# First pair's queries fetched from ScalarE's queue beside its keys; the gate values fetched and computed behind them

## The chip, the core and the metric

The kernel runs on one core of a Trainium2 chip. The metric is device time in microseconds (us), the median of several runs. An engine is named as in the profile: PE (TensorE), DVE (VectorE), ACT (ScalarE), POOL (GpSimd) and SP (SyncE), of which SP only issues transfers here. ACT can issue transfers too, between its computations.

## What is computed

One attention layer (4 batches, 8 heads, 576 positions, 64 wide) with a memory term and a gate for each head, and behind it two feed-forward layers with 2,304 tokens, 512 to 2,048 to 512.

```python
def _attn_ref(q, k, v, M_prev, z_prev, beta):
    scores = scale * np.matmul(q, k.transpose(0, 1, 3, 2))     # causal mask, softmax -> a
    local = np.matmul(a, v)
    q_p = phi(q)
    mem_out = einsum('bhsd,bhde->bhse', q_p, M_prev) / (einsum('bhsd,bhd->bhs', q_p, z_prev)[..., None] + 1e-06)
    g = 1.0 / (1.0 + np.exp(-beta))[None, :, None, None]
    return g * mem_out + (1 - g) * local
# then x @ w_in -> elu -> @ w_out, then x @ w2_in -> leaky relu -> @ w2_out
```

## The kernel before

**Work.** A pair is two heads of one batch, so there are 16 pairs, four to a batch. For each pair the kernel loads keys, queries and values as natural rows (`load_qk`, `load_rest`; tiles `kn`, `qn`, `vn`, one buffer each), transposes keys and queries on PE (`k_unit` line 294, `q_unit` line 312), and copies them out of PSUM on ACT (lines 296 and 241) and DVE (line 243). Two head-items of a pair, each in two groups of rows (chunks 0 and 1, then 2 to 4), go through scores (PE line 426, in later batches 428 and 429), mask and row minimum (DVE 431), exponential (ACT 436), normalisation (POOL 445 and 451, DVE 446), transposes of the weights (PE 457, copied out by ACT into `d`, `ah`, `ac`), and the product with the values (PE 524). `phi_unit` makes the memory term from `qn` (ACT 385 and 386, DVE 387, POOL 389 and 396); it needs `ging`, and POOL 451 needs `omg`, both made from the gate input `beta`. The first batch is computed in full-precision matmuls, the others in split high and low parts.

**Weights.** The feed-forward weights come as 64-bit numbers (`wraw`, lines 103 and 107, 512 KB each, two buffers) and are decoded by ACT (113, later 127), DVE (114 to 122, later 128 to 132), an ACT cast (241, `w`) and a subtraction. Seven blocks of the first layer are decoded beside the first batch's attention.

**Filling.** When a batch is done, its feed-forward part (PE 620 and 648) is laid between the attention units of the next batch. After the last attention unit the rest of it, the remaining weight blocks and then the second half of layer one and layer two follow. At that handover `u_x` makes the input of the next part: DVE adds the two halves (681), ACT rounds them in four pieces (`xh`, 610), POOL makes the remainders (`xl`, 613). PE's first matmul on that part waits for one ACT count, that of the fourth piece.

**Order.** The code writes units in a fixed order, and a scheduler then orders the instructions of each engine, once, when the program is built. Transfers carry one of eight counters in turn (printed `DMAHW0` to `DMAHW7`), and a transfer waits until the one before it on its counter has landed. So a transfer that moves at the start renumbers those behind it.

**Start.** SP issues `beta`, four transfers of keys, four of queries, then values and weights. ACT loads its function table and makes `ging` (line 84); DVE makes `ging`, `gat`, `omg` (85 to 87).

Of the kernel before, what the change touches and what calls it, by code (L numbers as in the profile page):

```python
# [11 lines left out]
AF = mybir.ActivationFunctionType  # L12
ALU = mybir.AluOpType
AX = mybir.AxisListType

P = 128
# [8 lines left out]
def kernel(  # L25
# [14 lines left out]
    nc = tc.nc  # L40
# [38 lines left out]
    bet = const.tile([P, H], F32, name="bet")  # L79
    gat = const.tile([P, H], F32, name="gat")  # L80
    ging = const.tile([P, H], F32, name="ging")
    omg = const.tile([P, H], F32, name="omg")
    nc.sync.dma_start(bet, beta.partition_broadcast(P))
    nc.scalar.activation(out=ging, in_=bet, func=AF.Exp, scale=-1.0)
    nc.vector.tensor_scalar(out=ging, in0=ging, scalar1=1.0, scalar2=None, op0=ALU.add)
    nc.vector.reciprocal(gat, ging)
    nc.vector.tensor_scalar(out=omg, in0=gat, scalar1=-1.0, scalar2=1.0, op0=ALU.mult, op1=ALU.add)


    wi_tiles = {}  # L90
    wo_tiles = {}
# [57 lines left out]
    def halves(n):  # L149
# [18 lines left out]
        out=mask[:, 448:576], in_=mask[:, 448:576], pattern=[[-1, 128]], compare_op=ALU.is_ge,  # L168
# [37 lines left out]
    def bank(tag):  # L206
        return psum.tile([P, 512], F32, tag=tag, bufs=BANKS[tag], name=tag)

    def load_rows(dst, src, b, hp, dup):

        hs = slice(2 * hp, 2 * hp + 2)
        for ca, cb, r0 in ((0, 2 if dup else 3, 0), (3, 5, 320)):
            for j in range(2):
                nc.sync.dma_start(
                    dst[:, ca:cb, j * D:(j + 1) * D],
                    src[b, 2 * hp + j, r0:r0 + (cb - ca) * P, :].rearrange("(c p) d -> p c d", p=P),
                )
        for r in range(2 if dup else 0):
            nc.sync.dma_start(
                dst[64 * r:64 * r + 64, 2, :].rearrange("p (j d) -> p j d", j=2),  # L220
                src[b, hs, 256:320, :].rearrange("j p d -> p j d"),
            )
# [29 lines left out]
    class Pair:  # L252
# [12 lines left out]
        def load_qk(self):  # L265
            self.q = at.tile([P, 5, P], F32, tag="qn", bufs=1, name="qn")
            self.k = at.tile([P, 5, P], F32, tag="kn", bufs=1, name="kn")
            load_rows(self.k, k, self.b, self.hp, False)
            load_rows(self.q, q, self.b, self.hp, False)

        def load_rest(self):
            b, hp = self.b, self.hp
            self.v = at.tile([P, 5, P], F32, tag="vn", bufs=1, name="vn")
            load_rows(self.v, v, b, hp, True)
            if hp % 2 == 0:
                load_memory(b, 2 * hp)
            zb, mr = memory_in[b, hp]
            h0 = 2 * (hp % 2)
            self.z = zb[:, h0 * D:h0 * D + P]
            self.mr = mr[:, h0:h0 + 2, :]  # L280
# [262 lines left out]
    def weave(*lists):  # L543

        keyed = []
        for n, (kind, l) in enumerate(lists):
            keyed += [((i + 0.5) / len(l) + SHIFT[kind], n, i, u) for i, u in enumerate(l)]
        return [u for _, _, _, u in sorted(keyed, key=lambda e: e[:3])]

    def attention_units():  # L550

        pairs = [Pair(ti, hp) for ti in range(len(tiles1)) for hp in range(NHP)]
        keys = [(pr, j, g) for pr in pairs for j in range(2) for g in pr.groups]
        items = [Item(*key, n) for n, key in enumerate(keys)]
        first = {}
        for n, it in enumerate(items):
            first.setdefault(id(it.pr), n)
        units = [(0, pairs[0].load_qk, None), (0, pairs[0].load_rest, None)]
        def prep(pi):
            pr = pairs[pi]  # L560
            l = [(PC, lambda g=g: pr.k_unit(g)) for g in pr.kgroups]
            l += [(PC, lambda g=g: pr.q_unit(g)) for g in pr.groups]
            l += [(0, pr.phi_unit)]
            if pi + 1 < len(pairs):
                l.append((0, pairs[pi + 1].load_qk))
            return l

        units += [(c, u, None) for c, u in prep(0)]
        for n in range(len(items) + 2):
            lists = []  # L570
            if n < len(items):
                it = items[n]
                pr = it.pr
                pi = pairs.index(pr)
                head = []
                if first[id(pr)] == n:
                    head.append((0, pr.v_unit))
                    if pi + 1 < len(pairs):
                        head.append((0, pairs[pi + 1].load_rest))
                if n + 1 < len(items) and items[n + 1].pr is not pr:  # L580
                    lists.append(("prep", prep(pi + 1)))
                lists.append(("score", head + it.stages()[0]))
            if 1 <= n <= len(items):
                lists.append(("tr", items[n - 1].stages()[1]))
            if n >= 2:
                it = items[n - 2]
                c = list(it.stages()[2])
                if first[id(it.pr)] == n - 2:
                    c = [(PC, lambda g=g, pr=it.pr: pr.qp_unit(g)) for g in it.pr.groups] + c
                lists.append(("pv", c))  # L590
            w = weave(*lists)
            done = None
            if n >= 2 and (n == len(items) + 1 or items[n - 1].pr.ti != items[n - 2].pr.ti):
                done = items[n - 2].pr.ti
            units += [(c, u, None) for c, u in w[:-1]] + [(w[-1][0], w[-1][1], done)]
        return units
# [143 lines left out]
    def close_mlp():  # L740
# [9 lines left out]
        NW, NG, EB = TW, 3, 2  # L750

    att = attention_units()
    n0 = [d for _, _, d in att].index(0) + 1
    c0 = sum(c for c, _, _ in att[:n0])
# [198 lines left out]
```

## Time and profile before

| what | value |
|---|---|
| median of 3 runs | 1080.63 us (1078.21 to 1080.70) |
| profiled execution | 1078.67 us, of which the span is 1076.9 us |
| PE busy | 1042.8 us, 97% of the span |
| DVE, ACT, POOL busy | 55%, 45%, 49% |
| transfers | 115.05 MB, mean 107 GB/s |

Times in the rows further down are microseconds from the span's start. In a timeline row the first number is the start and the second the duration; a bracket at the end gives how long the engine stood idle before it and who released it. In a row of a stretch, each engine has its busy time and, in parentheses, its instructions; then come the clock granted to PE (1.00 is full), the mean busy share of the transfer engines, and GB/s.

### The profile page before, as it was taken

The page shows a single profiled execution, that of the slowest core. Times are in us where ns is not written, and L with a number is a line of the kernel's source. Part 1 is how long each engine was busy: PE and PEld are TensorE (multiplying, and loading weights), DVE is VectorE, ACT ScalarE, POOL GpSimd, SP SyncE. Part 2 cuts the span into 40 slices and gives each one's busy share as a digit, 9 for nine tenths or more (in the row PEclk, how much of TensorE's full clock was granted, in tenths as well). Part 3 has the DMA queues.
Part 4 walks back from the last instruction along what each step waited for, and adds up shares of the span by engine and source line. Part 5 has one row for each costly group of instructions (what it writes and reads, how often), then busy time and mean ns, then how long its engine had stood idle before and what let it go on. Part 6 is the DMA issues. An engine that isn't in the chain of part 4 may idle for free.

```text
span 1076.9 us, 17323 instructions
## 1 busy us (share of the span) xinstructions
PE 1042.8 (97%) x5904; PEld 912.1 (85%) x5904; DVE 589.7 (55%) x1382; ACT 484.3 (45%) x1169; POOL 529.9 (49%) x674
## 2 busy tenths in 40 slices
PE   6998999999999998999999999999999999999997
PEld 3776799989999998988888889888888888888896
DVE  6889987788878647566672214654322221232232
ACT  5999877778877634544442224432211211111111
POOL 6676775677667525654542225954422422222221
PEclk9999999999999998999999999999999999999999
DMA  7755553564446247765671304430200100000010
GB/s 182 197 145 117 161 142 101 122 169 145 114 120 161 90 134 240 251 226 179 201 224 61 117 1 134 160 118 1 79 1 1 59 20 1 10 30 1 1 40 20
DMA packets 150408, 115.05 MB, mean 107 GB/s; under 512 B 80048, under 2 KB 142000, under 8 KB 150320
## 3 DMA queue, kind: packets, MB, share of 16 engines
q1 hardware_dynamic: 150320, 113.94, 35.9%
q8 instruction: 47, 0.77, 0.3%
q14 instruction: 41, 0.34, 0.1%
HBM read 78.52 MB, written 31.85 MB: 102 GB/s over the span
## 4 chain that ended last, share of the span: by engine, by line
PE 81%; DVE 8%; DMA 5%; ACT 2%; issue 2%; POOL 1%; SPq 1%; DVEq 0%; POOLq 0%; ACTq 0%
PE pm L620 18%; PE tp L620 15%; PE sc L901 14%; PE sc L648 10%; PE pm L648 4%; PE po L901 4%; PE tp L457 3%; PE po L524 3%; PE po L648 3%; PE pm L524 2%; DVE pt L431 2%; PE sc L426 1%; DMA y<-xq 1%; PE sc L428 1%; PE sc L429 1%
## 5 line engine op out<-in xcount | busy, mean ns | idle before, releaser
L627 POOL TENSOR_TENSOR gl<-e,gh 128x512 fp32r<-128x512 f32 (+2 forms) x181 | 200.8, 1112 | 384.5 <-DVE gh L243 267.4
L620 PE MATMUL tp<-xw,w 128*128 128x512 f32 (+1 forms) x504 | 144.3, 367 | 0.0
L620 PE MATMUL pm<-xw,w 128*128 128x512 f32 (+1 forms) x496 | 141.9, 369 | 0.0
L901 PE MATMUL sc<-w,gh 128*128 128x512 f32 x448 | 135.9, 390 | 0.0
L451 POOL TENSOR_SCALAR pt<-pt,rs,omg 128x128 f32<-128x128 f32 (+4 forms) x160 | 102.1, 647 | 22.1 <-DVE rs L446 17.9
L620 PEld LDWEIGHTS tp<-xw,w 128*128 128x128 f32 x504 | 91.8, 188 | 16.1
L648 PE MATMUL sc<-gh,w 128*128 128x512 f32 (+2 forms) x438 | 104.8, 340 | 0.0
L620 PEld LDWEIGHTS pm<-xw,w 128*128 128x128 f32 x496 | 90.6, 188 | 16.3
L436 ACT ACTIVATE pt<-pt,mx 128x128 f32<-128x128 f32 (+4 forms) x160 | 93.3, 585 | 17.2 <-DVE mx L431 16.3
L901 PEld LDWEIGHTS sc<-w,gh 128*128 128x128 f32 x448 | 83.1, 188 | 16.5
L620 PE MATMUL tp<-xv,w 128*128 128x512 f32 (+1 forms) x252 | 92.6, 367 | 0.0
L620 PE MATMUL pm<-xv,w 128*128 128x512 f32 (+1 forms) x248 | 91.4, 369 | 0.0
L639 ACT ACTIVATE e<-pm 128x512 f32<-128x512 f32 (+1 forms) x40 | 22.2, 555 | 143.2 <-PE pm L620 140.2
L457 PE MATMUL tp<-ident,pt 128*128 128x128 f32 x480 | 81.6, 279 | 2.8 <-ACT ah L247 0.9
L901 PE MATMUL sc<-w,gl 128*128 128x512 f32 x224 | 84.3, 389 | 0.0
L640 DVE TENSOR_TENSOR e<-tp,e 128x512 f32<-128x512 f32 (+1 forms) x40 | 25.5, 637 | 106.3 <-ACT e L639 106.3
L648 PEld LDWEIGHTS sc<-gh,w 128*128 128x128 f32 x438 | 74.8, 188 | 8.6
L138 POOL TENSOR_TENSOR w<-wm,w 128x512 fp32r<-128x512 f32 x50 | 65.5, 1331 | 33.1 <-ACT w L241 22.1
L640 DVE TENSOR_TENSOR e<-pm,e 128x512 f32<-128x512 f32 (+1 forms) x40 | 25.5, 637 | 101.8 <-ACT e L639 101.8
L620 PE MATMUL pm<-xh,w 128*128 128x288 f32 x368 | 80.6, 306 | 0.3 <-DVE e L634 0.3
L243 DVE CAST gh<-e 128x512 fp32r<-128x512 f32 (+2 forms) x146 | 72.9, 503 | 12.7 <-PE po L901 2.2
L639 ACT ACTIVATE e<-tp 128x512 f32<-128x512 f32 (+1 forms) x40 | 22.1, 554 | 117.7 <-PE tp L620 112.2
(157 smaller groups left out, 2444.1 us busy)
## 6 DMA issues: line engine op xcount, KB each, us to landing
wraw<-in_moe_w_in_dram SPq DMA_DIRECT2D x32, 512.0 KB, 4.0
wraw<-in_moe_w_out_dram SPq DMA_DIRECT2D x32, 512.0 KB, 5.2
xh<-xh SPq DMA_DIRECT2D x8, 576.0 KB, 3.1
xl<-xl SPq DMA_DIRECT2D x8, 576.0 KB, 3.8
ys<-st SPq DMA_DIRECT2D x32, 144.0 KB, 2.8
x<-x1s SPq DMA_DIRECT2D x9, 512.0 KB, 3.9
out_dram<-st SPq DMA_DIRECT2D x36, 128.0 KB, 1.7
vn<-in_v_dram SPq DMA_DIRECT2D x64, 64.0 KB, 2.3
```

The source lines that it names most:

```text
L138: nc.gpsimd.tensor_tensor(out=w[:, 1, a], in0=t[:, a], in1=_f(w)[:, 0, a], op=ALU.subtract)
L243: (nc.vector if eng == "V" else nc.gpsimd).tensor_copy(dst, src)
L436: nc.scalar.activation(out=pt[0:m, 0:nk], in_=pt[0:m, 0:nk], func=AF.Exp, scale=-1.0, bias=mx[0:m, last:last + 1], accum_out=self.pd["ss"] ...
L451: nc.gpsimd.tensor_scalar(out=pt, in0=pt, scalar1=rs[0:m, i:i + 1], scalar2=omg[0:m, h:h + 1], op0=ALU.mult, op1=ALU.mult,)
L457: nc.tensor.transpose(dst, self.p[c][:, k0:k0 + kn], ident)
L524: nc.tensor.matmul(po[:, a:b], w, x, start=i == 0, stop=i == len(mms) - 1)
L620: nc.tensor.matmul(ph, wi[:, wj, kc, :], xx[:, kc, :], start=n_mm == 0, stop=n_mm == 11)
L627: nc.gpsimd.tensor_tensor(out=gl, in0=g, in1=_f(gh), op=ALU.subtract)
L639: nc.scalar.mul(t, ph, 0.01)
L640: nc.vector.tensor_tensor(out=t, in0=ph, in1=t, op=ALU.max)
L648: nc.tensor.matmul(py, wo[:, wj, ec * P:(ec + 1) * P], gg, start=opens and f == first and n_mm == 0, stop=closes and f == last and n_mm == 2,)
L901: nc.tensor.matmul(pos[tb], gg[:, tb * P:(tb + 1) * P], wo[:, wj, :], start=f == 0 and n_mm == 0, stop=f == NF - 1 and n_mm == 2,)
```

## The change

`load_rows` takes the issuing engine as an argument, and the first pair's queries use ACT's. The gate block becomes a function, which the list of units calls between `load_qk` and `load_rest` of the first pair. No arithmetic is added or removed, and every engine has the instructions it had, except that four transfers go from SP to ACT. Since line numbers move by one behind the gate block, line 215 of the kernel after is line 214 of the kernel before, and so on.

```diff
-    nc.sync.dma_start(bet, beta.partition_broadcast(P))
-    nc.scalar.activation(out=ging, in_=bet, func=AF.Exp, scale=-1.0)
-    nc.vector.tensor_scalar(out=ging, in0=ging, scalar1=1.0, scalar2=None, op0=ALU.add)
-    nc.vector.reciprocal(gat, ging)
-    nc.vector.tensor_scalar(out=omg, in0=gat, scalar1=-1.0, scalar2=1.0, op0=ALU.mult, op1=ALU.add)
-
+
+    def gates():
+        nc.sync.dma_start(bet, beta.partition_broadcast(P))
...
-    def load_rows(dst, src, b, hp, dup):
+    def load_rows(dst, src, b, hp, dup, eng=nc.sync):
...
-                nc.sync.dma_start(
+                eng.dma_start(
...
-            load_rows(self.q, q, self.b, self.hp, False)
+            load_rows(self.q, q, self.b, self.hp, False, nc.sync if self.ti or self.hp else nc.scalar)
...
-        units = [(0, pairs[0].load_qk, None), (0, pairs[0].load_rest, None)]
+        units = [(0, pairs[0].load_qk, None), (0, gates, None), (0, pairs[0].load_rest, None)]
```

The scheduler puts out another order from the start on, on every engine, up to the early part of what follows the attention; PE's order is the same from its instruction 3,389 of 5,786 on.

First place: SP at the start of the program. Before:

```order
L83 DMA bet<-in_beta_dram 128x8
L214 DMA kn<-in_k_dram 128x3x64 x2
L214 DMA kn<-in_k_dram 128x2x64 x2
L214 DMA qn<-in_q_dram 128x3x64 x2
L214 DMA qn<-in_q_dram 128x2x64
L214 DMA qn<-in_q_dram 128x2x64 [waits DMAHW0_49]
L214 DMA vn<-in_v_dram 128x2x64 [waits DMAHW1_49]
L103 DMA wraw<-in_moe_w_in_dram 128x4x256 [waits DMAHW2_49]
```

SP at the same place, after:

```order
L215 DMA kn<-in_k_dram 128x3x64 x2
L215 DMA kn<-in_k_dram 128x2x64 x2
L85 DMA bet<-in_beta_dram 128x8 [waits DMAHW0_49]
L104 DMA wraw<-in_moe_w_in_dram 128x4x256 [waits DMAHW1_49]
L108 DMA wraw<-in_moe_w_out_dram 128x1024 [waits DMAHW2_49]
L215 DMA vn<-in_v_dram 128x2x64 [waits DMAHW3_49]
```

The queries have left SP; `beta` now waits on the counter of the first query transfer (counters 0 and 3 are those that the first query transposes on PE wait for), and the weights stand ahead of the values. PE's transposes of query chunks 0 to 2 now stand between those of key chunks 0 to 2 and those of key chunks 3 and 4; before, all keys came first.

Second place: ACT where it first copies transposed weights `ah` out of PSUM, some 27 us into the span before. In it, `po<-wraw` opens the decoding of half a weight block and `CAST w` ends it. Before:

```order
L113 ACTIVATE po<-wraw 128x512 [waits DMAHW2_49,DVE_49]
L436 ACTIVATE pt_515,ss_149<-pt_515,mx 128x128 [waits DVE_49,Pool_49]
L436 ACTIVATE pt_526,ss_149<-pt_526,mx 128x256 [waits DVE_49,Pool_49]
L241 CAST w_391<-po 128x512 [waits DVE_49]
L247 COPY ah<-tp 128x320 [waits PE_49] x2
```

ACT at the same copies, after:

```order
L529 COPY xp<-pm 64x256 [waits PE_49]
L114 ACTIVATE po<-wraw 128x512 [waits DMAHW2_49,DVE_49]
L248 COPY ah<-tp 128x320 [waits PE_49] x2
L463 COPY d_146<-tp 128x384 [waits PE_49]
L242 CAST w_391<-po 128x512 [waits DVE_49]
```

The two copies of `ah` now stand ahead of the cast that ends that half block.

Third place: ACT at the handover behind the attention, some 400 us into the span. Before:

```order
L241 COPY st<-sc 128x288 [waits DMAHW2_49,PE_49]
L241 COPY st<-sc 128x288 [waits DMAHW4_49,PE_49]
L610 CAST xh_6579<-x 128x288 [waits DMAHW3_49,DMAHW7_49,DMAHW1_49,DVE_49]
L610 CAST xh_6579<-x 128x288 [waits DVE_49] x2
L127 ACTIVATE wm<-wraw 128x1024 [waits DMAHW5_49,DMAHW6_49,DMAHW2_49,DMAHW1_49]
L241 COPY st<-sc 128x288 [waits DMAHW0_49,PE_49,Activation_49]
L241 COPY st<-sc 128x288 [waits DMAHW1_49,PE_49,Activation_49]
L610 CAST xh_6579<-x 128x288
L241 CAST w_6660<-wm 128x1024 [waits DVE_49]
```

ACT at the same handover, after:

```order
L611 CAST xh_6579<-x 128x288 [waits DMAHW3_49,DMAHW7_49,DMAHW1_49,DVE_49]
L611 CAST xh_6579<-x 128x288 [waits DVE_49] x2
L128 ACTIVATE wm<-wraw 128x1024 [waits DMAHW5_49,DMAHW4_49,DMAHW6_49,DMAHW2_49,DMAHW1_49]
L242 COPY st<-sc 128x288 [waits PE_49]
L242 COPY st<-sc 128x288 [waits DMAHW4_49,PE_49]
L242 CAST w_6660<-wm 128x1024 [waits DVE_49]
L242 COPY st<-sc 128x288 [waits DMAHW5_49,PE_49,Activation_49]
L242 COPY st<-sc 128x288 [waits DMAHW6_49,PE_49,Activation_49]
L611 CAST xh_6579<-x 128x288
```

The fourth `xh` piece, on which PE's next matmul waits, now stands behind four `st` copies and the weight cast instead of two `st` copies. On PE the last product of the last attention unit stands 25 matmuls earlier than before (instructions 2,435 to 2,445 where it was 2,460 to 2,470).

## Rows read from the trace of the kernel before

**Rows 1.** The page, part 1: busy time, share, instructions of each engine
```profile
PE 1042.8 (97%) x5904; PEld 912.1 (85%) x5904; DVE 589.7 (55%) x1382; ACT 484.3 (45%) x1169; POOL 529.9 (49%) x674
```

**Rows 2.** Stretches: PE, weight loads, DVE, ACT, POOL, clock, transfer share, GB/s
```profile
4.00:8.00 4.00, 3.26 (x12) 2.13 (x13) 1.25 (x2) 1.83 (x5) 3.71 (x10) 1.00 0.70 150
8.00:16.00 8.00, 6.67 (x24) 3.78 (x23) 7.41 (x26) 6.43 (x18) 5.28 (x11) 1.00 0.79 225
16.00:27.00 11.00, 8.15 (x36) 4.27 (x34) 8.62 (x24) 6.14 (x20) 6.64 (x14) 1.00 0.81 204
27.00:54.00 27.00, 26.13 (x150) 21.51 (x150) 23.47 (x65) 25.60 (x70) 17.73 (x33) 1.00 0.71 197
```

**Rows 3.** Sum of 25 stretches of 2 us from 80 to 130 us
```profile
sum 50.00, PE 44.46 PEld 36.12 DVE 47.61 ACT 44.38 POOL 33.18; mean PE 1.78 PEld 1.44 DVE 1.90 ACT 1.78 POOL 1.33
```

**Rows 4.** Timeline of SP: the transfers issued in the first 21 us
```profile
0.72 0.39 SPq L83 DMA_DIRECT2D bet<-in_beta_dram  x1
...
1.17 1.99 SPq L214 DMA_DIRECT2D kn<-in_k_dram  x4
3.20 2.04 SPq L214 DMA_DIRECT2D qn<-in_q_dram  x4
...
6.86 0.47 SPq L107 DMA_DIRECT2D wraw<-in_moe_w_out_dram  x1
...
12.60 1.96 SPq L214 DMA_DIRECT2D kn<-in_k_dram  x4
...
20.05 0.59 SPq L103 DMA_DIRECT2D wraw<-in_moe_w_in_dram  x1
```

**Rows 5.** Half a microsecond while only keys and `beta` are in flight, as Rows 2
```profile
3.00:3.50 0.50, 0.00 (x0) 0.00 (x0) 0.00 (x0) 0.20 (x1) 0.46 (x2) 1.00 0.99 223
```

**Rows 6.** Transfers issued from 0 to 14 us: KB each, us to landing
```profile
wraw<-in_moe_w_in_dram SPq DMA_DIRECT2D x1, 512.0 KB, 4.0
wraw<-in_moe_w_out_dram SPq DMA_DIRECT2D x1, 512.0 KB, 5.7
```

**Rows 7.** Timeline of the start: table load, transposes, first mask operations
```profile
0.72 1.28 ACT L84 ACT_TABLE_LOAD   x1 [0.72 <-PEq L937]
...
4.15 0.88 PE L294 MATMUL sc<-ident,kn 128*128 128x128 f32 x3 [4.15 <-DMA kn<-in_k_dram]
...
4.84 0.37 ACT L296 COPY kk<-sc 128x256 f32<-128x256 f32 x1 [1.34 <-PE sc L294]
...
6.28 1.46 PE L312 MATMUL sc<-ident,qn 128*128 128x128 f32 x5 [0.35 <-DMA qn<-in_q_dram]
...
8.29 0.29 DVE L431 CUSTOM_DVE_ANT_0 pt<-sc,mask 128x128 f32<-128x128 f32 x1 [0.49 <-PE sc L426]
```

**Rows 8.** Timeline from 24 to 28 us: weight decoding and the copies of `ah`
```profile
24.04 0.65 ACT L113 ACTIVATE po<-wraw 128x512 f32<-128x512 f32 x1 [2.75 <-DMA wraw<-in_moe_w_in_dram]
...
27.40 0.76 ACT L247 COPY ah<-tp 128x320 f32<-128x320 f32 x2
```

**Rows 9.** The handover, 387 to 414 us: stretches, then timeline rows
```profile
387.00:396.00 9.00, 9.00 (x70) 9.00 (x69) 5.40 (x13) 3.13 (x8) 4.80 (x6) 1.00 0.40 100
...
405.00:414.00 9.00, 7.73 (x38) 7.74 (x39) 3.89 (x6) 3.89 (x8) 4.10 (x4) 0.62 1.07 314
...
399.80 1.57 DVE L681 TENSOR_TENSOR x<-x,y 128x288 f32<-128x288 f32 x4 [6.88 <-DMA y<-xq]
...
403.27 1.12 ACT L127 ACTIVATE wm<-wraw 128x1024 f32<-128x1024 f32 x1 [1.44 <-DMA wraw<-in_moe_w_out_dram]
405.08 0.80 ACT L241 COPY st<-sc 128x288 f32<-128x288 f32 x2 [0.69 <-DMA ys<-st]
405.78 0.43 ACT L610 CAST xh<-x 128x288 fp32r<-128x288 f32 x1
408.20 1.05 ACT L241 CAST w<-wm 128x1024 fp32r<-128x1024 f32 x1 [1.99 <-DVE wm L132]
...
406.27 0.85 PE L620 MATMUL tp<-xh,w 128*128 128x288 f32 x2 [4.21 <-ACT xh L610]
```

More of the change, by code (lines that the diff above doesn't have):

```diff
@@ L82 @@
     omg = const.tile([P, H], F32, name="omg")
-    nc.sync.dma_start(bet, beta.partition_broadcast(P))
-    nc.scalar.activation(out=ging, in_=bet, func=AF.Exp, scale=-1.0)
-    nc.vector.tensor_scalar(out=ging, in0=ging, scalar1=1.0, scalar2=None, op0=ALU.add)
-    nc.vector.reciprocal(gat, ging)
-    nc.vector.tensor_scalar(out=omg, in0=gat, scalar1=-1.0, scalar2=1.0, op0=ALU.mult, op1=ALU.add)
+    def gates():
+        nc.sync.dma_start(bet, beta.partition_broadcast(P))
+        nc.scalar.activation(out=ging, in_=bet, func=AF.Exp, scale=-1.0)
+        nc.vector.tensor_scalar(out=ging, in0=ging, scalar1=1.0, scalar2=None, op0=ALU.add)
+        nc.vector.reciprocal(gat, ging)
+        nc.vector.tensor_scalar(out=omg, in0=gat, scalar1=-1.0, scalar2=1.0, op0=ALU.mult, op1=ALU.add)
     wi_tiles = {}
```

## The prediction

> **What bounds the kernel now.** I read the page first: PE is busy for 1042.8 of 1076.9 us [rows 1], so 34 us at most can be won without less PE work. The next view is busy time by stretch, to see where those 34 us lie. From 27 to 54 us PE is busy 26.13 of 27 us; up to 27 us it is not, and the reader should add up the gaps there: nothing runs before 4.15 us [rows 7], and the next three stretches lack 0.74, 1.33 and 2.85 us [rows 2], 9.1 us together. Two more places stand out. From 80 to 130 us DVE is busy 47.61 of 50 us and PE 44.46 [rows 3]: here DVE sets the pace. At the handover behind the attention PE stands 4.21 us and then finds a granted clock of 0.62 of full speed, the mean over 9 us [rows 9]; that is, having stood, it gets the lower of its two levels (1.2 of 2.4 GHz) for most of them. What the change touches on purpose lies in the first 27 us; there I read timelines, engine by engine.
>
> What ends last in these 27 us? First keys, then queries: PE's key transposes start at 4.15 us when keys land, its query transposes at 6.28 us when queries land, the first mask operation on DVE at 8.29 us [rows 7]. Then SP. Its queue issues one transfer after the other, about half a microsecond each, and it comes to the second weight block only at 20.05 us [rows 4]. That block lands at 24.04 us; ACT has waited 2.75 us for it, with the copies of `ah` queued behind it until 27.40 us [rows 8]. PE's gapless stretch begins there.
>
> **The change part by part.**
>
> *Gate load off the head of SP.* The first key transfer is issued at 0.72 instead of 1.17 us [rows 4]: 0.45 us earlier.
>
> *Queries on ACT's queue.* Four issues of 2.04 us together [rows 4] leave SP and run beside the keys. Do keys and queries land earlier? With keys alone in flight the transfer engines are already busy 0.99 of the time, at 223 GB/s [rows 5]. Two queues therefore share that rate. The four first transfers (keys and queries, chunks 0 to 2) are 96 KB each, 0.39 MB, and take 1.8 us at 223 GB/s; before, half of that was ready for PE at 4.15 us, some 3.0 us after its first issue. I take the same latency plus the 0.9 us for the other half, less 0.45: both land near 4.2 to 4.6 us. So keys gain nothing, and the first queries gain 6.28 less some 4.5, 1.7 us.
>
> *ACT before its first copy.* Four issues at 0.5 us each from 0.72 us end at 2.8; the table load of 1.28 us ends at 4.0; the first copy of keys is at 4.84 us [rows 7]. What hides the issues is ACT's wait for the first transposes; 0.8 us of it are left. Without that cover, two microseconds would go onto the path. The Trainium skill ("ScalarE: Activation LUTs", section "What ACT_TABLE_LOAD costs") adds a drain of about 1.4 us to a load of about 1.3 us; the trace shows the 1.28 us, and no row here shows a drain. By that page ACT would be ready at 5.4 us, and the start would gain some 0.5 us less.
>
> *Gate values later.* The gate transfer now waits until a query transfer has landed (some 3.5 us) and lands itself 2.5 us later, near 6 us. In ACT's order `ging` stands ahead of the copies of the later key and query chunks, in DVE's order ahead of the first mask operation. So ACT goes on at about 6.5 us and DVE's first mask operation is at about 7.0 instead of 8.29 us: gain 1.3, not 1.7.
>
> *SP behind it.* Without four query issues SP is 2.04 us ahead. It gives some back: its transfers wait for counters, and `mr` now waits for the first weight block. Before, the second pair's keys waited for that block: issued at 6.86 us, 5.7 us to landing, 12.56, and keys at 12.60 [rows 4, 6]. Now it goes out at about 4.3 us behind the counter waits and lands near 10.0; the two `mr` take about 1 us behind it, and keys follow at some 10.8 to 11.2. So the queue is 1.4 to 1.8 us ahead there, and the second weight block goes out at about 18.4 instead of 20.05 us, to land 4.0 us later [rows 6], near 22.4 instead of 24.04.
>
> *ACT at 27 us.* In the new order the copies of `ah` wait for the first decode step of that block (0.65 us, so 23.1 us) and no longer for the cast that ends it, which stood behind three DVE steps. They could then run at about 24.0 instead of 27.40 us. The gain at this point is bounded by 0.9 us (only DVE's chain gains, less what sharing the transfer rate costs) and 3.4 us (27.40 less 24.0). I take 2.0: the weight block gains 1.7, and the nearest bound on the rest is the reordering, of which I count a little. Behind it PE lacks 0.87 of 27 us up to 54 us [rows 2], so there is hardly a gap to lose the gain in, and what follows shifts as a whole.
>
> *The handover.* Of the reordering, this is the one place where a row carries a price. PE's 4.21 us end with the fourth `xh` piece at 405.78 us [rows 9]. In the new order it stands behind the weight cast as well. That cast comes 3.8 us after the end of the decode step that opens it (404.39 to 408.20) and takes 1.05; two `st` copies of 0.80 follow. With the weights landing as before, the piece would run at about 410.05 instead of 405.78: 4.3 us more. Against that, the last product of the attention stands 25 matmuls earlier on PE, 3.2 us at 9.00/70 us each [rows 9], and with it the transfers through which `x` reaches DVE (399.80) and the weights that are issued behind them. If both shift by the whole 3.2 us, the piece runs 1.0 us later than before. With the shift spread over a transfer path that is full (share 1.07), I take 1.0 us lost, with bounds of 1.5 us won (the weights of that load gain more than `x`) and 4.3 us lost.
>
> *All other order.* PE's order differs in most of its first 3,389 instructions. No unit is added, and the copies of an engine are the same ones. I take it as nothing, with 2.5 us to either side: half of what PE lacks from 80 to 130 us, 5.5 us [rows 3], which is where DVE is nearly full and a swapped operation counts.
>
> *Sum.* 2.0 won, 1.0 lost: 1.0 us off the profiled execution of 1078.67, so 1077.7; the 1.8 us of it that lie outside the span stay. This execution lies 2.0 us under the median of the runs, 1080.63. I forecast the median: 1079.6 us.
>
> **The rivals.**
>
> *The start gives all and the handover closes.* 3.4 us at the start and 1.5 at the handover give 1075.7 us. For it: three queues of waits (SP, ACT at 24 us, queries) shorten together. Against it: it needs the new order to be kind at a place where ACT has more in front of the piece.
>
> *ACT holds PE at the handover (slower).* One mechanism: the fourth `xh` piece behind the weight cast. It decides from the point where the weight block lands less than 1 us earlier against PE than before; then PE's stand grows towards 8.5 us. With 0.9 us won at the start and 4.3 lost this is 1084.0 us. For it: ACT's order as printed, and a transfer share of 1.07 there, under which a block cannot hurry. Against it: the 25 matmuls.
>
> *Nothing is hidden that was not hidden before.* The keys already fill the transfer engines [rows 5], so a second queue moves no byte sooner; only 0.45 us for the gate load is won, and 1080.2 us result. The row of 0.99 speaks for it, the 20.05 us at which SP gets to the weights against it. The Trainium skill says it as a rule ("DMA: Bandwidth & Descriptors", section "Issuing engines are not separate DMA queues"): transfers from all engines run on the same 16 and interleave, and several issuers save only the time to issue. The trace agrees as to the rate; the issue time is here what SP runs out of.
>
> **How the numbers follow.** A difference of 0.3%, 3.2 us, is about what a measurement of this kernel can tell from no change. The forecast case gets 0.42, the idle change 0.10: both lie within 3.2 us, so 0.52 for the same. The full gain gets 0.27, faster. The handover gets 0.21, slower. The range leaves out the outer part of the two last cases, and takes the 2.5 us of the remaining order: 1075.0 to 1084.0 us.
>
> **What would show it.** At the start: query transposes on PE at about 4.5 to 5 us, the first mask operation near 7.0 us, second keys on SP near 11 us, second weights near 18.4 us, and `ah` copies near 24 to 25 us. A busy share of PE that is 2 us higher up to 27 us confirms the first term. If the second weights go out on SP at 20 us again, the first term is wrong. At the handover: the fourth `xh` piece behind a weight cast, and PE standing about 5 us; 8 us would show the slower rival, under 3 us the faster one. The stretch from 80 to 130 us should show PE at 44.5 of 50 us again; several us more or less there would mean that the order alone, and not the start, made the time.

## The result, and the profile after

The changed kernel takes 1092.35 us (median of 4 runs, 1091.37 to 1094.02) where the kernel before takes 1079.42 (1077.89 to 1080.70): a ratio of 1.012, with an interval from 1.0105 to 1.0136. It is 12.9 us slower. The forecast was 1079.6 us, no measurable change, with a range up to 1084.0; the time lies outside it. The profiled execution of the changed kernel took 1094.02 us, of which the span is 1092.2.

The page of after, part 1, answers [rows 1]:

```profile
PE 1048.6 (96%) x5904; PEld 917.4 (84%) x5904; DVE 592.1 (54%) x1382; ACT 483.8 (44%) x1169; POOL 530.4 (49%) x674
```

The span grew by 15.3 us. PE is busy 5.8 us longer for the same instructions, and idle 9.5 us longer. The first thing to look at is the start, which the change is about. The stretches of after, with the columns of [rows 2], and under them the sum of 25 stretches of 2 us from 80 to 130 us, which answers [rows 3]:

```profile
4.00:8.00 4.00, 3.49 (x13) 2.79 (x14) 1.13 (x6) 2.53 (x8) 3.71 (x10) 1.00 0.80 211
8.00:16.00 8.00, 7.08 (x26) 4.41 (x26) 7.71 (x26) 5.93 (x19) 6.66 (x15) 1.00 0.76 192
16.00:27.00 11.00, 9.17 (x48) 6.50 (x46) 8.66 (x24) 8.75 (x26) 6.85 (x10) 1.00 0.76 196
27.00:54.00 27.00, 24.34 (x137) 19.15 (x136) 21.05 (x63) 21.86 (x61) 17.38 (x32) 1.00 0.56 157
...
sum 50.00, PE 43.49 PEld 34.69 DVE 46.35 ACT 41.52 POOL 33.30; mean PE 1.74 PEld 1.39 DVE 1.85 ACT 1.66 POOL 1.33
```

Up to 27 us PE has done 19.74 us of work where it had done 18.08: the start is better by 1.7 us. By 54 us that is gone: the stretch that was gapless, 26.13 of 27 us [rows 2], now has 24.34. Nothing of the 13 us is lost in the first 27 us, and the rest is lost far from what the diff touches.

Where, a table shows. For every stretch of 6 us I take PE's idle time, and what a clock below 1.00 took from its busy time (busy time times one less the granted clock), and add them up. Microseconds of PE lost, by part of the span; the kernels from e1 on are those of the experiments:

| kernel | 0 to 54 | 54 to 132 | 132 to 216 | 216 to 252 | 252 to 402 | 402 to 540 | sum |
|---|---|---|---|---|---|---|---|
| before | 9.8 | 8.6 | 0.9 | 2.7 | 3.6 | 8.2 | 33.7 |
| after | 9.9 | 9.7 | 2.4 | 7.6 | 6.5 | 11.6 | 47.7 |
| e3 | 8.8 | 8.7 | 1.1 | 2.7 | 4.2 | 7.9 | 33.4 |
| e4 | 10.9 | 9.2 | 2.3 | 7.8 | 4.9 | 13.3 | 48.3 |
| e5 | 9.6 | 9.6 | 8.5 | 7.5 | 5.7 | 8.4 | 49.3 |
| e6 | 8.1 | 8.8 | 2.4 | 3.8 | 5.6 | 8.5 | 37.1 |
| e7 | 9.8 | 8.8 | 1.5 | 3.4 | 7.0 | 13.4 | 43.9 |
| e8 | 7.6 | 14.5 | 1.3 | 3.9 | 4.2 | 7.1 | 38.5 |
| e9 | 8.6 | 9.1 | 1.3 | 2.7 | 3.6 | 6.4 | 31.6 |

Of the 14.0 us between before and after, 9.6 are idle time and 4.3 are clock. Behind the start both kernels lose most where one batch's attention ends and the next begins (near 100, 215, 325 and 405 us). After also loses where before loses hardly anything: 2.6 us from 30 to 48, 1.2 from 138 to 150 and 4.5 from 240 to 258 us, against 0.3 of before in all three. These sums belong to one profiled execution each.

### The profile page after: what moved, and what is told of

Same layout as the page of the kernel before. It is cut to its first block, busy times and chain, and to the rows that moved or that the text cites. A ratio compares the mean times of both kernels' runs of the same rounds, so it can differ in the third digit from the quotient of the medians.

```text
span 1092.2 us, 17383 instructions
## 1 busy us (share of the span) xinstructions
PE 1048.6 (96%) x5904; PEld 917.4 (84%) x5904; DVE 592.1 (54%) x1382; ACT 483.8 (44%) x1169; POOL 530.4 (49%) x674
## 4 chain that ended last, share of the span: by engine, by line
PE 77%; DVE 8%; DMA 5%; ACT 3%; POOL 3%; issue 2%; SPq 1%; DVEq 0%; POOLq 0%; ACTq 0%
PE pm L621 18%; PE tp L621 14%; PE sc L902 14%; PE sc L649 8%; PE po L902 4%; PE pm L649 4%; PE po L525 3%; PE tp L458 3%; PE po L649 3%; PE pm L525 2%; PE sc L427 1%; PE sc L429 1%; PE sc L430 1%; DMA wraw<-in_moe_w_out_dram 1%; POOL w L139 1%
## 5 line engine op out<-in xcount | busy, mean ns | idle before, releaser
L437 ACT ACTIVATE pt<-pt,mx 128x128 f32<-128x128 f32 (+4 forms) x160 | 93.3, 585 | 21.1 <-DVE mx L432 18.4
L649 PEld LDWEIGHTS sc<-gh,w 128*128 128x128 f32 x438 | 75.8, 191 | 11.6 <-ACT st L242 2.7
```

Of the source, the lines that this page charges most:

```text
L437: nc.scalar.activation(out=pt[0:m, 0:nk], in_=pt[0:m, 0:nk], func=AF.Exp, scale=-1.0, bias=mx[0:m, last:last + 1], accum_out=self.pd["ss"] ...
L649: nc.tensor.matmul(py, wo[:, wj, ec * P:(ec + 1) * P], gg, start=opens and f == first and n_mm == 0, stop=closes and f == last and n_mm == 2,)
```

## The experiments

**Is it the change, or the order?** The build's scheduler ordered all instructions anew. To part the two, e3 and e4 hold the order: a table in the kernel lists, for each engine, the instructions in the wanted order, and each is tied behind its predecessor by an edge that sets issue order only. The five gate instructions and the first four query transfers are left free. e3 makes the whole change and holds the order of before; e4 makes none of it and holds the order of after.

```diff
+FREE = {45, 46, 47, 48, 63, 64, 65, 66, 67}
+ORDER = (
...
+)
+def pin(tc, nc):
+    ins = [i for n, i in enumerate(nc.cur_bb.bb.instructions) if n not in FREE]
...
+        for x, y in zip(row[:-1], row[1:]):
+            tc.add_manual_dep(
+                ins[y], ins[x].name, mb.DependencyInfo(mb.DependencyClass.NoSync, mb.DependencyReason.DATA), reason="pin"
+            )
```

> The whole change is made (first queries on ScalarE's queue, gate values behind them), but every other instruction is held, engine by engine, in the order in which it stands in the kernel before (the build's own scheduler had put 1184 of the 5784 TensorE instructions of the changed kernel elsewhere). Theory 'order': the change itself gains the 2 to 4 us seen up to 31 us and the loss comes from the other order alone, so this run takes 1075 to 1079 us, against 1079.4 before. Rival 'cost': the new queue or the later gates cost the 13 us by themselves (semaphores, ScalarE's issues, later weights), so this run stays near 1092. Rival 'both': near 1084 to 1086.

> The change is not made (queries on SyncE's queue, gate values first, as before), but every other instruction is held in the order of the changed kernel. Theory 'order': the loss is here in full without the change, and the start gains nothing: 1092 to 1097 us. Rival 'cost': near 1079. Rival 'both': 1084 to 1088.

e3 took 1078.68 us, ratio to before 0.9994 (0.9983 to 1.0004). e4 took 1093.86, ratio 1.0148 (1.0119 to 1.0177). The traces bear out the edits: e3 runs PE, DVE and POOL in exactly the sequence of before, and PE of e4 that of after. The change in the old order costs nothing that can be measured; the new order without the change costs everything. In the table, e4 loses where after loses. The rival that the queue or the gates cost by themselves is out.

**The halves of the change.** Each in the order that the scheduler gives it. e1 is the change with the gate block at its old place; e2 is the change with this line put back:

```diff
-            load_rows(self.q, q, self.b, self.hp, False, nc.sync if self.ti or self.hp else nc.scalar)
+            load_rows(self.q, q, self.b, self.hp, False)
```

> Only the first queries go to ScalarE's queue; the gate values stay where they were; the scheduler orders the rest anew (984 of 5784 TensorE instructions stand elsewhere than before). Theory 'order': a third order, whose time has nothing to do with the part of the change that is made: anywhere in 1075 to 1095 us, and the differences of the two halves do not add up to 12.9 us. Rival 'cost' with the queue as its cause: near 1092; with the gates as its cause: near 1079.

> Only the gate values are fetched and worked on behind the first queries; all queries stay on SyncE's queue; the scheduler orders the rest anew (1029 of 5784 TensorE instructions stand elsewhere than before). Theory 'order': a fourth order, anywhere in 1075 to 1095 us. Rival 'cost' with the gates as its cause: near 1092; with the queue as its cause: near 1079, and the two halves together make 12.9 us.

e1 took 1086.61 us, 1.0064 (1.0045 to 1.0083), e2 1091.53, 1.0118 (1.0098 to 1.0137): 7.5 and 12.4 us, 19.9 together, not 12.9. They are not parts of a sum but two more orders.

**Is a new order as often better?** e14 to e16 change something else, small, on the kernel before, so that the scheduler orders anew. e13 is the counterpart: it moves a single transfer, and every other instruction keeps its place.

```diff
-    nc.sync.dma_start(bet, beta.partition_broadcast(P))
+    nc.scalar.dma_start(bet, beta.partition_broadcast(P))
```

```diff
-        nc.sync.dma_start(zb, z_prev[b, h0:h0 + 4, :].rearrange("h d -> (h d)").partition_broadcast(P))
+        (nc.sync if h0 or b else nc.scalar).dma_start(zb, z_prev[b, h0:h0 + 4, :].rearrange("h d -> (h d)").partition_broadcast(P))
```

```diff
-            load_rows(self.v, v, b, hp, True)
             if hp % 2 == 0:
                 load_memory(b, 2 * hp)
+            load_rows(self.v, v, b, hp, True)
```

```diff
-    RESERVE = 60000.0
+    RESERVE = 60500.0
```

> Only the fetch of the gate values (bet) goes to ScalarE's queue; every other instruction keeps its place on its engine. SyncE's first issue is then that of the keys: about 0.45 us earlier. Theory 'the start is worth little': within 0.6 us of before at the end (1078.4 to 1079.6). Rival 'what SyncE gains at the start is kept': 0.4 to 1 us faster.

> Only the first load of zb (one issue of 0.59 us at 9 us) goes to ScalarE's queue; the scheduler puts 974 of 5784 TensorE instructions elsewhere. Theory 'a favourable order was left': slower than before, 1082 to 1094 us. Rival 'a new order is as often better': even odds of being below 1079.

> The loads of zb and mr are written ahead of those of the values vn, for all pairs; the scheduler puts 1178 of 5784 TensorE instructions elsewhere. Theory 'a favourable order was left': slower than before, 1082 to 1094 us. Rival 'a new order is as often better': even odds of being below 1079.

> Only the planner's constant RESERVE is 60500 instead of 60000, so that the fill work is handed out 0.3 per cent more slowly; nothing at the start changes; 1016 of 5784 TensorE instructions stand elsewhere. Theory 'a favourable order was left': slower than before, 1081 to 1094 us. Rival 'a new order is as often better': even odds of being below 1079.

e13: 1079.50 us, 0.9993 (0.9984 to 1.0003). e14: 1085.41, 1.0050 (1.0031 to 1.0070). e15: 1094.44, 1.0138 (1.0123 to 1.0153). e16: 1090.36, 1.0095 (1.0077 to 1.0113). With after, e1 and e2 that makes six new orders, all slower, by 5 to 14 us in the medians and some 10 on average; if a new order were as often better as worse, six of six would come up once in 64. They are six orders and not one: between any two of them some 1,800 to 2,460 of PE's first 3,450 matmuls are of another kind at the same place in the traces. So the order of before is a favourable one, and an edit that gives it up pays for that. How before came by its order no run shows. And only for the change itself (e3, e4) is the edit parted from its order: e14 to e16 were not run with the order held.

**Where in the order?** e5 and e6 make the change and hold a mixed order: e5 that of after up to PE's 1075th instruction (about 190 us) and then that of before; e6 that of before, but that of after between the 1075th and the 1590th (about 190 to 262 us). Only the table `ORDER` differs from e3's.

> The change is made. Every engine follows the order of the changed kernel up to TensorE's 1075th instruction (about 190 us), then the order of the kernel before. From the sums of PE's idle time and clock loss: up to 216 us the changed kernel had lost 22.0 us against 18.7 with the order of before (e3). Theory 'place by place' (each place where the order is worse costs its own, and nothing is carried on): 1078.7 + 3.3 = 1082 us (1080.5 to 1083.5). Rival 'carried on' (an early disorder spoils everything behind it): 1088 or more. Rival 'late order alone': 1079.

> The change is made. Every engine follows the order of the kernel before, except between TensorE's 1075th and 1590th instruction (about 190 to 262 us), where it follows the changed kernel's. Between 216 and 252 us the changed kernel lost 7.5 us and e3 2.7. Theory 'place by place': 1078.7 + 4.8 = 1083.5 us (1081 to 1085). Rival 'carried on' (that stretch is bad only because of what came earlier): 1079.

e6: 1083.83 us, 1.0038 (1.0025 to 1.0051), 5.2 us over e3 and within the forecast. But the forecast took these microseconds from 216 to 252 us, where after loses 7.6, and there e6 loses 3.8, only 1.1 more than e3, and nothing to the clock. The rest is spread over other columns, and two seams between orders are in it. So the time agrees in part by luck: the stretch with its seams costs some 5 us, but it does not repeat the worst place of after. e5: 1091.41, 1.0112 (1.0092 to 1.0132), far from the forecast 1082. The table shows why: 8.5 us at the seam (132 to 216 us) and 7.5 behind it. The timeline of e6, DVE, and of e5 at the seam, DVE and PE:

```profile
200.08 1.20 DVE L682 TENSOR_TENSOR x<-x,y 128x288 f32<-128x288 f32 x3 [2.28 <-DMA y<-xq]
...
214.47 1.20 DVE L682 TENSOR_TENSOR x<-x,y 128x288 f32<-128x288 f32 x3 [6.61 <-DMA vn<-in_v_dram]
...
217.04 0.58 PE L525 MATMUL po<-qph,ms 128*128 128x256 f32 x1 [6.28 <-DVE qpl L251]
```

DVE stands for 6.61 us in front of the additions `x<-x,y`, because in the mixed order they come up before the batch's attention, whose result they add, is back: its reload `y` goes out at 209.72 us and takes 4.7 us to land (the trace names `vn`, issued behind it). All scores queue behind them, and PE stands 6.28 us. Behind the stand the clock took another 4.0 us up to 252 us. So e5 measured its own seam and left its question open, but it pointed at the additions. In e6 DVE stands in front of them at 200 us, where before does too, and not at 214 us, where after does.

**What stands in the worst stretch?** The stretches of after, and under them those of before:

```profile
216.00:222.00 6.00, 3.38 (x23) 2.87 (x22) 5.67 (x13) 5.04 (x15) 5.83 (x9) 0.96 0.20 57
222.00:228.00 6.00, 5.92 (x38) 5.51 (x37) 5.78 (x16) 3.78 (x11) 2.50 (x7) 0.75 0.66 187
...
240.00:246.00 6.00, 3.99 (x21) 4.02 (x21) 3.34 (x11) 4.40 (x12) 4.37 (x6) 0.72 0.04 8
```

```profile
216.00:222.00 6.00, 5.14 (x39) 4.35 (x38) 5.73 (x18) 4.88 (x16) 5.31 (x10) 1.00 0.42 125
222.00:228.00 6.00, 4.50 (x32) 3.69 (x32) 5.69 (x18) 5.68 (x15) 2.91 (x5) 1.00 0.58 151
```

In after PE is busy 3.38 of 6 us and then gets a clock of 0.75; in before it has 5.14 and keeps 1.00. The timeline of after around the gap, DVE, ACT and PE:

```profile
211.07 0.48 DVE L251 TENSOR_TENSOR al<-tp,ah 128x320 fp32r<-128x320 f32 x1
214.17 1.20 DVE L682 TENSOR_TENSOR x<-x,y 128x288 f32<-128x288 f32 x3 [2.61 <-DMA y<-xq]
215.28 0.42 DVE L432 CUSTOM_DVE_ANT_0 pt<-sc,mask 128x256 f32<-128x256 f32 x1
...
217.94 2.36 DVE L388 SCALAR_TENSOR_TENSOR ph_f<-qn,ph_e 128x640 f32<-128x640 f32 x1 [0.25 <-ACT ph_e L387]
220.23 0.41 DVE L532 COPY xp<-po 128x256 f32<-128x256 f32 x1
...
214.66 1.17 ACT L611 CAST xh<-x 128x288 fp32r<-128x288 f32 x3 [2.36 <-DVE x L682]
...
215.77 0.44 PE L295 MATMUL sc<-ident,kn 128*128 128x128 f32 x2 [0.97 <-DVE mx L432]
...
220.79 0.39 PE L525 MATMUL po<-qph,ms 128*128 128x320 f32 x1 [2.50 <-ACT kk L301]
```

The same additions, and this time in a kernel that nobody mixed. Three of them, for chunks 1 to 3 of the next feed-forward part, wait for a reload; ACT's three copies `xh` wait for them; the mask operation of a score comes 3.7 us behind the end of the operation ahead of them (211.55 to 215.28 us). The additions of before, and the wait on PE that follows, DVE and PE of its timeline:

```profile
200.92 1.20 DVE L681 TENSOR_TENSOR x<-x,y 128x288 f32<-128x288 f32 x3 [2.06 <-DMA y<-xq]
...
202.71 0.33 PE L428 MATMUL sc<-kk,qs 128*128 128x128 f32 x1 [0.78 <-DVE qs L343]
```

DVE stood 2.06 us there as well. But at 201 us PE had feed-forward matmuls of the part before to run, up to 214.7 us, and lost 0.78 us; in after the last of them starts at 214.42 us. Why three run ahead: the code pins chunk 0, with the addition and the copy, behind what its engine was given before (`keep_in_program_order`), and leaves chunks 1 to 3 free. So chunk 0, the piece that PE waits for, comes last, as at the handover that the prediction spoke of. e7 is after in its own order with nine instructions moved: the three additions, copies and remainders go behind those of chunk 0.

> The changed kernel in its own order, with 9 instructions moved: at about 214 us the three additions x<-x,y of chunks 1 to 3 go behind that of chunk 0 (225 us) on VectorE, likewise their three copies xh on ScalarE and the three subtractions xl on GpSimd. Theory 'VectorE stands': VectorE's 2.61 us and ScalarE's 2.36 us before these, in which they wait for the reload y<-xq while scores wait behind them, are what makes PE idle for 0.97 and 2.50 us and drops its clock to 0.75: 1092.4 - 3 to 5 = 1087 to 1090 us. Rival 'TensorE's own order': the wait at 220.8 us is named for the copy kk and stays: 1091.5 to 1093.

e7 took 1089.10 us, 1.0085 (1.0068 to 1.0102) to before: 3.3 us less than after. Its timeline, DVE and PE:

```profile
215.28 0.81 DVE L388 SCALAR_TENSOR_TENSOR ph_f<-qn,ph_e 128x640 f32<-128x640 f32 x1
216.01 0.41 DVE L532 COPY xp<-po 128x256 f32<-128x256 f32 x1
...
220.87 1.56 DVE L682 TENSOR_TENSOR x<-x,y 128x288 f32<-128x288 f32 x4
...
216.57 0.39 PE L525 MATMUL po<-qph,ms 128*128 128x320 f32 x1 [0.63 <-DVE xp L532]
```

The four additions now run in one go with no wait. PE's 0.97 and 2.50 us have become 0.63 us, with 0.36 and 1.49 us new behind it (at 221.0 and 223.0 us), and from 216 to 252 us the table has 3.4 us instead of 7.6, of which the clock had taken 2.7 and now takes nothing. Over half of that gain, 2.4 us, lies behind 228 us, at additions that e7 did not move: DVE stands 0.59 us there instead of 2.10, and PE 0.59 instead of 2.12.

The wait of 2.50 us, which the trace names for the copy `kk`, was DVE's, as forecast, but not all of it was DVE's stand. In both kernels PE's matmul starts right behind DVE's copy `xp`, and that stands behind `ph_f`, which takes 2.36 us in after and 0.81 in e7. So 1.55 of the 2.50 us go with the length of `ph_f`, beside which POOL was at work in after and idle in e7. e7 moved three additions, three copies and three remainders at once; it shows that their place costs 3.3 us, and not which of the two, the stand or the long `ph_f`, has what share.

**Do such moves add up?** e9 takes e3 and, at the last two parts (400 and 420 us), puts chunk 0's copy and remainder, at 420 us its addition too, ahead of the others. e10 does that and e7's move at four places. e11 and e12 do the same to the order of after. All four leave out the two pins, which the table replaces:

```diff
-            if c == 0:
-                tc.keep_in_program_order(hi)
...
-                    if c == 0:
-                        tc.keep_in_program_order(add)
```

> The change in the order of the kernel before (e3), with 5 instructions moved and the two pins keep_in_program_order taken out: at the last two loads of attention's result (about 400 and 420 us) ScalarE's copy xh of chunk 0 goes ahead of those of chunks 1 to 3, and so ahead of wm and two copies st; GpSimd's xl likewise, and at 420 us VectorE's addition too. Theory 'chunk 0 stands behind its pin': TensorE's waits of 4.14 us (for xh, at 406.8) and of 1.50 us (for xl, at 431.1) go, and perhaps some of the 2.3 us of clock loss there: 1078.7 - 4 to 7 = 1071.5 to 1074.5 us. Rival 'another wait takes its place' (xl, a bank, the weights): 1077 to 1079.

> As e9, and at the four earlier loads of attention's result (about 200, 240, 303 and 340 us) the additions, copies and subtractions of chunks 1 to 3 go directly behind those of chunk 0, as in e7. Theory 'VectorE stands': VectorE's waits of 1.4 to 2.2 us in front of these additions go, and of what TensorE waits for scores there (0.98 us at 202.6, 0.68 at 307.7) some 1 to 2 us: 1 to 2 us below e9. Rival: these waits are covered by TensorE's other work: same as e9 within 0.7 us.

> The changed kernel in its own order with the same 5 instructions moved as in e9. Theory 'chunk 0 stands behind its pin': of TensorE's waits at the end of attention (2.51 us for st, 2.72 and 1.63 us for xh) the two for xh go: 1092.4 - 4 = 1088 us (1086 to 1089.5). Rival 'another wait takes its place': 1091 to 1093.

> As e11, and all four sets of chunks moved as in e10 (one of them is e7's, which took 3.3 us). Theory 'the chunks are the greater part of what the other order costs': 1092.4 - 4 - 3.3 - 1 to 3 = 1082 to 1084 us. Rival 'they are a part like others': 1085 to 1087.

e9: 1078.28 us, 0.9985 (0.9968 to 1.0002). e10: 1084.37, 1.0044 (1.0030 to 1.0057). e11: 1092.66, 1.0118 (1.0094 to 1.0143). e12: 1093.89, 1.0133 (1.0087 to 1.0180). Only e9 came out below its base, 0.4 us under e3 in the medians, where 4 to 7 us were expected, and its interval spans 1. e11 is as slow as after, e12 no faster, and e10, expected 1 to 2 us under e9, is 6 us above it. The timeline of e9, ACT, PE and POOL:

```profile
402.49 0.44 ACT L611 CAST xh<-x 128x288 fp32r<-128x288 f32 x1 [0.55 <-DVE x L680]
...
410.42 0.53 PE L619 MATMUL tp<-xh,w 128*128 128x288 f32 x2 [1.32 <-DVE e L633]
422.43 1.07 PE L647 MATMUL sc<-gh,w 128*128 128x288 f32 x6 [0.96 <-DVE gh L244]
428.11 0.40 PE L647 MATMUL sc<-gl,w 128*128 128x288 f32 x1 [2.75 <-POOL gl L626]
...
420.72 2.80 POOL L139 TENSOR_TENSOR w<-wm,w 128x512 fp32r<-128x512 f32 x2
423.48 2.84 POOL L612 TENSOR_TENSOR xl<-x,xh 128x288 fp32r<-128x288 f32 x3
426.29 1.77 POOL L626 TENSOR_TENSOR gl<-e,gh 128x288 fp32r<-128x288 f32 x1
```

The 4.14 us for `xh` are gone, and waits of 1.32, 0.96 and 2.75 us have come, the last for `gl` on POOL, which stands behind a weight subtraction and three remainders. "Another wait takes its place" is what happened. In e10 the four additions, run in one go, stand in front of DVE's work for scores at other places, for 1.56, 2.57 and 5.51 us (from 222, 326 and 355 us on): PE waits 1.93, 2.96 and 3.47 us there (at 224, 330 and 361 us), in e9 0.83, 0.87 and not at all. That the 13 us come from the order is therefore shown (e3, e4), and for 3 of them the nine instructions that bring them (e7); for the rest the cause stays open, and no single rule on these chunks mends it.

**The start, and a better version.** e8 takes e2's start, the best up to 84 us, and goes on in the order of before. e17 is e9 with the second weights issued ahead of the second pair's values. e18 is e9 once more, with more runs.

> Queries on SyncE's queue, gate values behind them (as in e2), in e2's own order up to TensorE's 360th instruction (about 80 us), then in the order of the kernel before. Up to 84 us e2 had lost 8.0 us of TensorE's time and the kernel before 9.9. Theory 'place by place': 1079.1 - 1.9 = 1077.2 us (1076 to 1078.5). Rival: the gain is given back at the next place where TensorE waits for others (as e3's 1.0 us at 54 us was 0.4 at the end): 1078.5 to 1079.5.

> As e9, and SyncE issues the second block of weights (wraw) ahead of the second pair's values instead of behind them, some 3.3 us earlier. Theory 'the copies ah wait for the second weights': ScalarE's wait of 2.40 us at 23.3 us and TensorE's of 1.94 us at 27.2 us go; if the gain is kept 1.5 to 2 us below e18, if later waits take it back (as with e8) the same as e18 within 0.7 us.

> e9 once more, in five rounds: 1.5 to 2 us below the kernel before (ratio 0.998 to 0.9995). Rival: no difference, the ratio's interval spans 1.

e8: 1084.75 us, 1.0048 (1.0033 to 1.0063), slower than either of its forecasts: its start is 2.2 us ahead of before at 54 us, and from there to 132 us it loses 5.9 us more than before. e2, which has no seam, loses 4.5 us more there; the cause was not followed. e17: 1079.40, 0.9997 (0.9986 to 1.0007), 1.5 us above e18 and so neither of its forecasts. e18: 1077.93 against 1079.73, 0.9983 (0.9972 to 0.9994): the change in the held order with five instructions moved beats both kernels, the one before by 1.8 us (0.6 to 3.0); what the change has in that and what the five moves have was not parted. The timeline of e17, ACT:

```profile
23.34 0.64 ACT L114 ACTIVATE po<-wraw 128x512 f32<-128x512 f32 x1 [0.89 <-DVE w L123]
...
26.68 0.76 ACT L248 COPY ah<-tp 128x320 f32<-128x320 f32 x2
```

The weights go out at 15.25 us, where e18 and e9 issue them at 18.31 and 18.85. The decode step waits for DVE instead and starts at the same 23.3 us as in e3 (below), later than in e18 and e9 (22.30 and 22.85); the copies `ah` are at 26.68 as in e3, where e18 and e9 have them at 25.64 and 26.20. Sooner weights alone bring nothing.

## Why the prediction was wrong, step by step

**The step that failed** is "All other order: I take it as nothing, with 2.5 us to either side". It measured 13.7 us with the change made (after against e3) and 14.8 without it (e4 against before), more than five times the margin and to one side only. Two things were wrong in it. The size was derived from one stretch, half of what PE lacks from 80 to 130 us; that stretch itself came to 43.49 instead of 44.46 us, a loss of 1.0, just as harmless as assumed. But the order changed up to instruction 3,389 and costs mostly at the places where a batch ends, and with the stands comes clock, 4.3 of the 14.0 us in the profiles. And the sign was taken as open, where six of six new orders were slower. The text's last sentence, that the order alone could make the time, named the right failure, but its sign for it, several us more or less from 80 to 130 us, did not show.

**The start** was right in most of its parts. The timeline of after, ACT, PE, DVE and SP, and above it a stretch with both queues in flight, answer [rows 4, 5, 7, 8]:

```profile
3.00:3.50 0.50, 0.00 (x0) 0.00 (x0) 0.00 (x0) 0.50 (x1) 0.46 (x2) 1.00 1.19 265
...
2.87 1.28 ACT L297 ACT_TABLE_LOAD   x1 [2.87 <-issue]
5.21 0.37 ACT L297 COPY kk<-sc 128x256 f32<-128x256 f32 x1 [1.06 <-PE sc L295]
25.66 0.75 ACT L248 COPY ah<-tp 128x320 f32<-128x320 f32 x2 [0.36 <-PE tp L458]
...
4.51 0.87 PE L295 MATMUL sc<-ident,kn 128*128 128x128 f32 x3 [4.51 <-DMA kn<-in_k_dram]
5.17 0.93 PE L313 MATMUL sc<-ident,qn 128*128 128x128 f32 x3
...
7.67 0.29 DVE L432 CUSTOM_DVE_ANT_0 pt<-sc,mask 128x128 f32<-128x128 f32 x1
...
11.15 2.11 SPq L215 DMA_DIRECT2D kn<-in_k_dram  x4
...
18.74 0.59 SPq L104 DMA_DIRECT2D wraw<-in_moe_w_in_dram  x1
```

- Keys and queries together: forecast 4.2 to 4.6 us; keys at 4.51, 0.36 later than before although issued 0.45 earlier, queries ready behind them at 5.17 at the latest. So the queues did share, but not the 223 GB/s of [rows 5], which the prediction took as the limit: with both in flight, 252 to 265 GB/s were moved from 2.5 to 4.0 us. And the first term, 0.45 us for the keys, is not there even when one queue has all of them: in e13 they are issued at 0.72 instead of 1.17 us, and PE starts on them at 4.17 instead of 4.15, and on the queries at 6.11 instead of 6.28.
- ACT hidden: right. The table load ends at 4.15, and the copy at 5.21 waited for PE. The Trainium skill ("ScalarE: Activation LUTs", section "What ACT_TABLE_LOAD costs") counts a drain of about 1.4 us as well; with it, as an estimate, ACT could not have begun before 5.5 us. The trace does not agree: ACT began at 5.21 us, right when PE's transposes were done, and in e3, with the load at the same place, at 5.03.
- First mask operation: 7.67 us, forecast 7.0, before 8.29. Half the gain.
- SP: second keys at 11.15 (forecast 10.8 to 11.2), second weights at 18.74 (18.4).
- `ah` at 25.66 instead of 24.0, before 27.40; what it waited for last was PE's transposes, and no longer the weights. PE's extra work up to 27 us was 1.7 of the 2.0 us taken. But "what follows shifts as a whole" was wrong: in after's order all of it was lost again by 54 us.
- One sum was off, and nothing hung on it: the gaps up to 27 us come to 8.9 us and not 9.1, since 0.15 us stood in two of its terms.

In the order of before the start is worth less: e3's timeline, DVE, ACT, PE and SP.

```profile
6.50 0.22 DVE L87 TENSOR_SCALAR ging<-ging 128x8 f32<-128x8 f32 x1 [4.78 <-ACT ging L86]
8.02 0.29 DVE L432 CUSTOM_DVE_ANT_0 pt<-sc,mask 128x128 f32<-128x128 f32 x1 [0.23 <-PE sc L427]
...
23.32 0.65 ACT L114 ACTIVATE po<-wraw 128x512 f32<-128x512 f32 x1 [2.40 <-DMA wraw<-in_moe_w_in_dram]
26.68 0.76 ACT L248 COPY ah<-tp 128x320 f32<-128x320 f32 x2
...
27.17 0.88 PE L458 MATMUL tp<-ident,pt 128*128 128x128 f32 x6 [1.94 <-ACT ah L248]
...
18.62 0.59 SPq L104 DMA_DIRECT2D wraw<-in_moe_w_in_dram  x1
```

The gate steps stand ahead of the first mask operation, which gains 0.27 us; SP's 1.43 us for the weights become 0.72 us at `ah`, since the block now takes 4.7 us to land; PE comes earlier and waits 1.94 us there instead of 0.87. PE is 1.0 us ahead at 54 us, and the time at the end differs by 0.4 us, within what can be measured. e13, the first term alone, is 0.8 us faster in the medians with a ratio of 0.9993 (0.9984 to 1.0003); that interval does not decide between its two forecasts.

**The handover** came out at the size that was forecast, but only in part by the mechanism. The timeline of after, ACT and PE, answers [rows 9]:

```profile
415.49 1.05 ACT L242 CAST w<-wm 128x1024 fp32r<-128x1024 f32 x1 [2.69 <-DVE wm L133]
418.68 0.79 ACT L242 COPY st<-sc 128x288 f32<-128x288 f32 x2 [2.14 <-DMA ys<-st]
419.37 0.43 ACT L611 CAST xh<-x 128x288 fp32r<-128x288 f32 x1
...
412.55 0.72 PE L649 MATMUL sc<-gh,w 128*128 128x288 f32 x2 [2.51 <-ACT st L242]
419.85 0.85 PE L621 MATMUL tp<-xh,w 128*128 128x288 f32 x2 [2.72 <-ACT xh L611]
441.14 0.53 PE L621 MATMUL pm<-xh,w 128*128 128x288 f32 x2 [1.63 <-ACT xh L611]
...
481.91 0.72 PE L621 MATMUL tp<-xw,w 128*128 128x512 f32 x2 [1.49 <-DVE e L635]
```

PE stands 2.51 and 2.72 us, 5.2 together, where it stood 4.21: the 1.0 us of the forecast. The fourth piece does run behind the weight cast, as forecast. But the cast is over at 416.54 us, and the two `st` copies in front of the piece then wait 2.14 us for a transfer; and PE's first 2.51 us end with an earlier `st` copy, not with the piece. Neither was in the sum, so its agreement is partly luck. Not forecast were the waits behind it, 0.57, 1.63 and 1.49 us, where before has one of 1.49: from 402 to 540 us after loses 11.6 us and before 8.2. The slower rival priced a stand of 8.5 us at one place; the time is slower for another reason.

**The rivals.** "The start gives all" fell with the start's gain by 54 us. "Nothing is hidden" (0.45 us and no more, 1080.2 us) comes near what the change does when the order is held (e3: 0.4 us in the medians), but not for its reasons: of the 0.45 us PE sees 0.17 at the queries and nothing at the keys (e13), the second queue did move bytes sooner (after), and PE of e3 is 1.0 us ahead at 54 us.

## What to carry to other kernels

Where a scheduler orders the program at build time, a small edit is two changes, the edit and a new order; hold the order, and measure each by itself. If the order before is the best of many that were tried, a new one is not an even bet: give it a cost of its own, here 5 to 14 us, larger than any term of the edit. And a stand of an in-order engine costs by what PE has left to do at that moment: 2.06 us on DVE cost PE 0.78 us with matmuls in store. Where there were none, 2.61 us on DVE, the long `ph_f` behind them and the clock after the gap went together, and moving nine instructions gave 3.3 us of the kernel's time back.

## What was not expected of the hardware

The clock falls at places that differ between executions of one and the same program, here on two chips. e9 and e18 are one kernel: up to 30 us the granted clock took 0.0 us from PE in the profile of e9 and 1.4 in that of e18, and from 84 to 132 us 3.0 and 1.2. e17 lost nothing to the clock up to 216 us, with 16.1 us of idle time, and e9 3.0 us with 15.9. So a clock loss of some 1.5 us at one place in one profile is not yet a property of the kernel, and the sums in the table are no finer than that.

The operation `ph_f` on DVE (128x640) has two kinds of duration. In before and after together it runs 32 times. In the 14 where POOL is at work for at most 0.14 us beside it, it takes 0.80 to 0.83 us; the 8 that take over 1.0 us, up to 2.36 at 217.94 us in after, all have POOL at work for at least 0.45 us of them. Ten others have POOL beside them for 0.27 us or more and still take 0.80 to 0.84. So what POOL does matters, and which of its operations was not tried. The 2.36 us lie in the worst stretch of after; in e7 the same operation has POOL idle beside it and takes 0.81. An addition `x<-x,y` of e10, which takes 0.45 us elsewhere, took 3.26 us at 357.04 us, with POOL at work for most of it.
